# An xLSTM cell and a feed-forward block on one core: float64 weights narrowed another way, the causal mask added by TensorE, and a new order for the first group

## The chip, the cores and the metric

The kernel runs on one core of a Trainium2 chip. The core has a matrix engine (TensorE, PE in the profile; its weight loads are PEld), a vector engine (VectorE, DVE), an activation engine (ScalarE, ACT), GpSimd (POOL) and a queue processor (SyncE, SP) which here does nothing but issue DMA requests. The metric is the device time of one execution in microseconds.

## The reference

Two blocks follow each other. The first is a recurrent cell (mLSTM) over 4 batches, 8 heads, 768 time steps and a head width of 40; the second is a feed-forward block over the 3072 tokens that come out of it:

```python
for t in range(S):
    m_new = np.maximum(f_gate[:, :, t] + m, i_gate[:, :, t])
    f_stab = np.exp(f_gate[:, :, t] + m - m_new)
    i_stab = np.exp(i_gate[:, :, t] - m_new)
    C = f_stab * C + i_stab * np.einsum('bhd,bhe->bhde', vt, kt)
    n = f_stab * n + i_stab * kt
    y[:, :, t] = sigmoid(o_gate) * (C q) / np.maximum(np.abs(n q), 1.0)
h = x @ w_in                 # x: 3072 x 320, w_in: 320 x 2048
g = np.maximum(0.01 * h, h)
return g @ w_out             # w_out: 2048 x 320
```

All inputs are float32 but the two weights, which arrive as float64. No engine computes in 64 bits, so the kernel takes each float64 apart by its bits and makes a float32 of it ("narrowing").

## The kernel before, in words

The 768 time steps are cut into six chunks of 128. A *step* s is one chunk of one batch (s = 4 c + b), 24 in all. Inside a chunk the recurrence is written as matrix products: scores k q, weighted by exponentials of the gate sums under a causal mask, times v. The feed-forward block runs over *groups*: group g takes the four steps of chunk g (512 tokens). The work of group 0 (the feed-forward of chunk 0) is woven between the cells of chunk 1, that of group 1 between the cells of chunk 2, and so on.

A float64 quarter of w_in (320 x 512, 1.31 MB) is one unit to load and narrow, n = 0 to 3; a unit of w_out (256 x 320, 0.66 MB) is n = 4 to 11. `load_weights` issues a quarter of w_in as ten requests (five slots of two halves of the partitions; L230) and a unit of w_out as one (L235). `narrow_weights` (L248) is seven steps: ACT takes the absolute value of the top 16 bits (Abs, L260); DVE clamps it (L262), shifts the exponent (L264), puts the sign back (L266), masks the low 20 bits of the high word (L271), adds the scaled low word (L275) and multiplies with the exponent (L277).

Each engine runs its instructions in the order in which they are written (`tc.manual_schedule` for PE, DVE, ACT and POOL); SP's requests follow in about the same order. The start is written out by hand, as a string of short commands (ORDER, L1102). The commands that matter here:

- `ld s`: load k, q and v of a step; `lo s`: its output gate; `lw n`: a weight unit; `fd s`, `ll s i`: loads for the steps of later chunks (k, v and the gate rows spread over the partitions; q and o).
- `g c`, `ge c`, `ug c`: gate scans of a chunk on DVE, their exponentials on ACT, their transposes on PE.
- `ab s`: PE spreads the gate sums of steps s and s+1 over all partitions into four PSUM banks (`spread_first`); `abw s`: DVE adds the causal mask and writes the sum to SBUF (`spread_mask`, L471); `exp s`: 8 exponentials on ACT (L488), one for each head.
- `tr s i`, `tc s i`: transposes of k and q on PE and their copies out of PSUM; `sc`, `scm`: scores on PE, and their product with the exponentials on DVE (L600); `st`, `stc`: state on PE and its copy (L616); `vu`: v times gate on POOL.
- `val`, `den`, `gate`, `gp`: values on PE (L673), their denominators on DVE, the output gate on DVE (L685), the scaling on POOL (L702); `o`: the tanh of the output gate on ACT.
- `x s`, `xc s`: transposes of a step's result on PE (L876) and four copies on ACT (L889, L890), which make the x of the feed-forward block.
- `ff i`: the i-th of 32 units of group 0's feed-forward block. Units 0 to 15 are products with w_in (L907), each with two leaky relus on ACT (L915); units 0 to 3 use quarter 0 of w_in, 4 to 7 quarter 1, and so on; 0 and 1 need the x of steps 0 and 1, 2 and 3 that of steps 2 and 3. Units 16 to 31 are products with w_out (L942); 16 to 19 need weight units 4 and 5, and so on.
- `nw n`: the next step of narrowing unit n. `ps`: memsets of a state tile on POOL.

After the string (from L1151) a loop runs the other 30 ff units. Before unit i it issues PASSES[i] further narrowing steps, then, by the list `place`, the cells of chunk 1: `u_split` (k and q transposed, PE L564, copied by ACT L570), `split_qs` (scaled q, PE L550, ACT L552), `u_parts` (scores and states, PE L650 and L655, DVE L660 and L632), `u_plain` (values, PE L713). `ahead` prepares the next step: `prep_exp`, `prep_qs` (POOL L517), the loads, `state_next` (POOL L628), `prep_vu` (POOL L508) and `prep_mask` (POOL L480). From group 1 on another plan goes on, which is not touched.

PSUM has eight banks: four tagged `mm` (gate spreads, the products with w_in and w_out) and four tagged `c` (all else). A product whose bank is still being read waits, and with it all of PE's later work.

## Time and profile before

| | |
|---|---|
| median of 3 runs | 489.19 us (488.82 to 491.32) |
| span of the profiled execution | 489.4 us |
| PE busy | 476.1 us (97%) |
| DVE busy | 365.9 us (75%) |
| ACT busy | 197.4 us (40%) |
| POOL busy | 160.3 us (33%) |
| mean granted clock of PE | 0.982 |

The profiled execution is one of its own: its span is the time from its first to its last instruction. Busy time of PE includes the wait of a pipelined product for its place, so a busy PE is not at its peak. In the page's slices of the span the granted clock of PE (tenths of full speed, a 40th of the span each) stands beside the busy share of PE:

```profile
PE   7969998999999999999999999999999999999997
...
PEclk9867999999999999999999999999999999999999
```

A row of the table of stretches reads: start and end (us), the length, then for PE, PEld, DVE, ACT and POOL the busy time and the number of instructions, the granted clock, the busy share of the DMA engines, and GB/s. A row of the timeline: start, duration, engine, line, operation, output and inputs with their shapes, and the count.

### The profile page before, as it was taken

Reading aid. Unit: us, or ns where it says so; the run is one execution under the profiler, and the core shown is the slowest. Engines: PE = TensorE matmul, PEld = TensorE weight load, DVE = VectorE, ACT = ScalarE, POOL = GpSimd, SP = SyncE. Lnnn points to the kernel's source line nnn. Section 1 sums busy time; section 2 is a strip of 40 time slices with the busy share of each in tenths; the row PEclk is TensorE's granted clock in tenths of the full one; section 3 lists DMA queues with packets and bytes.
Section 4 is the critical chain, followed back from the end, with each engine's and each line's share of the span. In section 5 each row is a group of like instructions: output and inputs, shape, how many; then the busy total and the mean of one; then the engine's idle time right before and its main releaser. Section 6 shows DMA issues by size and latency. Waiting matters only on the chain.

```text
span 489.4 us, 12856 instructions
## 1 busy us (share of the span) xinstructions
PE 476.1 (97%) x5137; PEld 377.9 (77%) x5137; DVE 365.9 (75%) x595; ACT 197.4 (40%) x510; POOL 160.3 (33%) x207
## 2 busy tenths in 40 slices
PE   7969998999999999999999999999999999999997
PEld 6857887777745479975559995557998889988997
DVE  5796999799924999777898777679899968335611
ACT  4674885453642240324342141425024752156310
POOL 4234454070600725817280563644220002100020
PEclk9867999999999999999999999999999999999999
DMA  7777686898623566668787877755151030100001
GB/s 136 177 191 146 161 226 134 216 229 177 143 97 90 133 158 176 162 152 202 152 197 160 189 181 177 184 144 153 44 229 42 1 107 1 42 15 0 1 1 54
DMA packets 142699, 63.41 MB, mean 130 GB/s; under 512 B 110832, under 2 KB 130864, under 8 KB 142640
## 3 DMA queue, kind: packets, MB, share of 16 engines
q1 hardware_dynamic: 142256, 62.47, 52.7%
q8 instruction: 40, 0.66, 0.6%
q14 instruction: 19, 0.16, 0.1%
q10 hardware_dynamic: 384, 0.13, 0.1%
HBM read 51.68 MB, written 8.27 MB: 122 GB/s over the span
## 4 chain that ended last, share of the span: by engine, by line
PE 82%; SPq 8%; DVE 5%; issue 2%; DMA 2%; ACT 1%; ACTq 0%; DVEq 0%
PE po L983 32%; PE ph L907 24%; PE ph L833 8%; PE po L942 6%; PE pe L833 4%; PE pT L743 3%; PE sd L650 3%; SPq L230 3%; SPq L368 2%; SPq L377 1%; PE sd L655 1%; DVE w_in L275 1%; PE hN L713 1%; DMA raw<-in_moe_w_in_dram 1%; DVE late L266 1%
## 5 line engine op out<-in xcount | busy, mean ns | idle before, releaser
L907 PE MATMUL ph<-xT,w_in 64*128 64x512 f32 (+1 forms) x800 | 146.3, 516 | 0.2 <-ACT xT L889 0.2
L907 PEld LDWEIGHTS ph<-xT,w_in 64*128 64x128 f32 x800 | 77.8, 190 | 57.4 <-issue 50.8
L983 PE MATMUL po<-w_out,acts 128*128 128x160 f32 x640 | 91.0, 301 | 0.0
L983 PEld LDWEIGHTS po<-w_out,acts 128*128 128x128 f32 x640 | 87.5, 190 | 3.4 <-ACT w L488 1.5
L915 ACT ACTIVATE acts<-ph 128x512 f32<-128x512 f32 (+1 forms) x80 | 36.8, 508 | 83.6 <-PE ph L907 83.5
L488 ACT ACTIVATE w<-w,gT 128x64 f32<-128x64 f32 (+1 forms) x192 | 52.0, 349 | 29.0 <-POOL w L480 28.0
L628 POOL TENSOR_TENSOR S<-S,f 40x336 f32<-40x336 f32 x36 | 32.5, 902 | 93.3 <-PE pT L743 49.5
L983 PE MATMUL po<-raw,acts 128*128 128x160 f32 x320 | 45.1, 299 | 0.0
L983 PEld LDWEIGHTS po<-raw,acts 128*128 128x128 f32 x320 | 44.0, 190 | 0.0
L660 DVE TENSOR_TENSOR qn<-w,sd 64x512 f32<-64x512 f32 x40 | 27.4, 684 | 21.0 <-PE sd L655 14.0
L1016 POOL TENSOR_TENSOR y<-y,raw 128x160 f32<-128x160 f32 x10 | 5.5, 555 | 112.3 <-ACT y L1015 112.3
L942 PE MATMUL po<-w_out,acts 128*128 128x320 f32 x128 | 36.0, 436 | 0.0
L855 DVE SCALAR_TENSOR_TENSOR acts<-ph,acts 128x512 f32<-128x512 f32 x32 | 20.6, 684 | 20.7 <-ACT acts L853 20.7
L541 DVE TENSOR_TENSOR qn<-kqT,late 64x512 f32<-64x512 f32 x32 | 33.1, 1033 | 1.0
L480 POOL TENSOR_TENSOR w<-w,i 128x512 f32<-128x512 f32 x20 | 31.8, 1591 | 2.7 <-ACT acts L915 1.9
L942 PEld LDWEIGHTS po<-w_out,acts 128*128 128x128 f32 x128 | 23.8, 190 | 9.5 <-issue 0.3
L757 POOL TENSOR_TENSOR xb<-xb,den 128x320 f32<-128x320 f32 x16 | 11.6, 727 | 48.7 <-DVE xb L754 48.7
L853 ACT ACTIVATE acts<-pe 128x512 f32<-128x512 f32 x32 | 17.4, 594 | 19.2 <-PE pe L833 19.0
L761 DVE STREAM_TRANSPOSE x<-xb 128x512 f32<-128x512 f32 x16 | 17.8, 1114 | 7.7 <-POOL xb L757 7.7
L859 ACT ACTIVATE acts<-acts 128x512 f32<-128x512 f32 x32 | 19.7, 633 | 8.0 <-DVE acts L855 8.0
L983 PE MATMUL po<-raw 128*128 128x160 f32 x160 | 22.7, 300 | 0.0
L650 PEld LDWEIGHTS sd<-kqT 40*64 40x64 f32 x640 | 19.7, 135 | 3.7 <-issue 3.0
(166 smaller groups left out, 773.2 us busy)
## 6 DMA issues: line engine op xcount, KB each, us to landing
w<-a_dr SPq DMA_DIRECT2D x40, 128.0 KB, 3.7
rb<-in_k_dram SPq DMA_DIRECT2D x64, 80.0 KB, 3.1
rb<-in_q_dram SPq DMA_DIRECT2D x64, 80.0 KB, 2.7
rb<-in_o_gate_dram SPq DMA_DIRECT2D x64, 80.0 KB, 2.6
xT<-x_dr SPq DMA_DIRECT2D x32, 160.0 KB, 3.2
late<-a_dr SPq DMA_DIRECT2D x32, 128.0 KB, 3.4
x_dr<-x SPq DMA_DIRECT2D x16, 256.0 KB, 3.4
kn<-in_k_dram SPq DMA_DIRECT2D x24, 160.0 KB, 3.7
```

What stands on the lines that cost most here:

```text
L480: nc.gpsimd.tensor_tensor(w, w, cm2.unsqueeze(1).to_broadcast([P, H, SL]), op=ALU.add)
L488: yield nc.scalar.activation(w[:, h, :], w[:, h, :], AF.Exp, bias=gT[c][:, 0, bh : bh + 1], scale=1.0)
L541: nc.vector.tensor_tensor(mixed(s)[rows, 1 - r], d["kqT"][rows, 1].rearrange("p (h t) -> p h t", t=SL), d["ea"][rows], op=ALU.mult,)
L628: nc.gpsimd.tensor_tensor(new, old, g, op=ALU.mult)
L650: nc.tensor.matmul(bank[1 - u][toks, h, :], lhsT=kqT[rows, 0, ts(h, SL)], rhs=kqT[rows, 1, ts(h, SL)], start=True, stop=True,)
L660: nc.vector.tensor_tensor(mixed(s)[toks, u], w[toks], bank[1 - u][toks], op=ALU.mult)
L833: nc.tensor.matmul(ph[r][:], lhsT=parts["w", key][n][part, at : at + P], rhs=xs[key][part, slot, :], start=start and slot == 0, stop=stop ...
L855: nc.vector.scalar_tensor_tensor(fs[r], in0=ph[r][:], scalar=1.0 + EPS, in1=fs[r], op0=ALU.mult, op1=ALU.add,)
L907: nc.tensor.matmul(ph[r][:, cols], lhsT=w_row(r, slot, j), rhs=xT[DP * r : DP * (r + 1), slot, bs, :], start=(slot == 0), stop=(slot == KC ...
L915: nc.scalar.activation(acts[:, f, cols], ph[r][:, cols], AF.Prelu, alpha=0.01)
L942: nc.tensor.matmul(po[n][:], lhsT=acts[:, f, ts(n, P)], rhs=w_out[:, f, :], start=(f == 0), stop=(f == NF - 1),)
L983: nc.tensor.matmul(bank[:], lhsT=left[:, f, :], rhs=right[:, f, :], start=f == 0, stop=f == KH - 1)
```

## The change

Four things are changed together.

1. *Loads of w_in.* A quarter is requested in two pieces, one for each half of the partitions, all five slots at once. `lw n half` names the half; units of w_out stay whole.
2. *Causal mask.* `mask_first` (`mk s`) writes the mask into the four gate banks by a bf16 product with a bf16 identity, and the spreads of the gate sums are accumulated on top. `spread_mask` is gone. ACT's exponentials read the banks in PSUM themselves, two heads for each command (`exp s g`).
3. *Narrowing.* Six commands for each unit. `na`: Abs on ACT, clamp on POOL (flag 1) or DVE (0). `nr`: the exponent's shift, on ACT as a scaled identity (1) or on DVE (0). `ns`: the sign, on DVE. `ng`: the low word scaled and 2^20 added, as float32, on ACT (1) or POOL (0), so that its bits are an integer field. `nm`: the middle 16 bits times 8 are added to that field's lower half as an integer, on DVE. `nc`: exponent and sign are added to the upper half as 16-bit integers, on DVE. The three full-width passes L271, L275 and L277 are thus replaced by one pass on ACT or POOL and two on DVE. On ACT are nr 1, 4, 5, 7, 11 and ng 0, 4, 7 to 11; on POOL the clamps of na 1, 2, 7, 9, 11 and ng 1, 2, 3, 5, 6.
4. *Order.* All of group 0 is now in the string; the loop with `PASSES`, `place` and `ahead` is gone. Copies can be sent to ACT or DVE by a flag (`tc`, `stc`, `xc`): five of eight transpose copies are now on DVE, five of eight state copies on ACT. New commands name what `ahead` did: `us` (u_split), `qs`, `lz` (begin the exponentials), `ex s n` (n of them), `sn` (state_next), `tq` (split_qs), `up` (u_parts), `upl` (u_plain), `pm` (prep_mask), `kq`, `sq`, `pv`, `fi`, `ux` (x and its copies).

```diff
-    cmask = consts.tile([P, P], F32, name="cmask")
+    cmask = consts.tile([P, P], BF16, name="cmask")
...
+    ident_b = consts.tile([P, P], BF16, name="ident_b")
+    nc.vector.tensor_copy(ident_b[:], ident[:])
...
-            for slot in range(KC):
-                for r in range(2):
-                    nc.sync.dma_start(
-                        to[DP * r : DP * (r + 1), 2 * P * slot : 2 * P * (slot + 1)], src[r, :, slot, :],
-                    )
+            for r in range(2) if half is None else (half,):
+                nc.sync.dma_start(
+                    to[DP * r : DP * (r + 1), :].rearrange("p (k c) -> p k c", k=KC), src[r],
+                )
...
+    def narrow_abs(n, on):
+        w = narrow(n)
+        top, tops = w["t"].bitcast(BF16), w["tops"].bitcast(BF16)
         nc.scalar.activation(top, tops, AF.Abs)
+        eng = nc.gpsimd if on else nc.vector
+        eng.tensor_scalar(top, top, scalar1=2.0**-15, scalar2=122368.0, op0=ALU.max, op1=ALU.min)
+
+    def narrow_exp(n, on):
+        w = narrow(n)
+        w["sign"] = 0x8000 if on else 0xC000
+        if on:
+            nc.scalar.activation(w["t"], w["t"], AF.Identity, bias=exp_bias[:], scale=8.0)
+        else:
+            nc.vector.tensor_scalar(
+                w["t"], w["t"], scalar1=0x07FF, scalar2=3, op0=ALU.bitwise_and, op1=ALU.logical_shift_left,
+            )
+
+    def narrow_sign(n):
+        w = narrow(n)
         nc.vector.scalar_tensor_tensor(
-            t, in0=tops.bitcast(U16), scalar=0xC000, in1=t, op0=ALU.bitwise_and, op1=ALU.bitwise_or,
+            w["t"], in0=w["tops"], scalar=w["sign"], in1=w["t"], op0=ALU.bitwise_and, op1=ALU.bitwise_or,
         )
...
+    def narrow_low(n, on):
+        w = narrow(n)
+        if on:
+            nc.scalar.activation(w["dst"], w["lo"], AF.Identity, bias=low_bias[:], scale=2.0**-32)
+        else:
+            nc.gpsimd.tensor_scalar(w["dst"], w["lo"], scalar1=2.0**-32, scalar2=2.0**20, op0=ALU.mult, op1=ALU.add)
+
+    def narrow_mid(n):
+        w = narrow(n)
+        nc.vector.scalar_tensor_tensor(
+            w["dst"].bitcast(U32), in0=w["mid"], scalar=8.0, in1=w["down"], op0=ALU.mult, op1=ALU.add,
         )
...
+    def narrow_join(n):
+        w = narrow(n)
+        nc.vector.tensor_tensor(w["up"], w["up"], w["t"], op=ALU.add)
...
+    def mask_first(s2):
+
+        ab = st["ab", s2] = [psf.tile([P, 2, H // RG, P], F32, name=f"ab{r}", tag="mm") for r in range(RG)]
+        by = cmask[:].unsqueeze(1).to_broadcast([P, 2 * H // RG, P])
+        for r in range(RG):
+            nc.tensor.matmul(ab[r][:].rearrange("p n m t -> p (n m) t"), lhsT=ident_b[:], rhs=by, start=True, stop=False)
...
-                        rhs=a[rows, :], start=True, stop=True,
+                        rhs=a[rows, :], start=False, stop=n == 1 and m == H // RG - 1,
...
+    def exp_first(s, g):
...
+        for h in range(2 * g, 2 * g + 2):
+            bh = s * H + h
+            nc.scalar.activation(
+                w[:, h, :], ab[h % RG][:, n, h // RG, :], AF.Exp, bias=gT[0][:, 0, bh : bh + 1], scale=1.0,
             )
...
     ORDER = """
-ld 0; warm 12; ld 1; ld 2; lo 0; lo 1; lo 2; lw 0
-g 0; ld 3; lw 1; lw 2; lo 3; ge 0; ug 0; tr 0 0
...
+warm 12; ld 0 0; ld 0 1; ld 1 0; mk 0; lo 1; ld 1 1; ld 1 2; g 0; tiles; ld 0 2; tr 0 0; ge 0; ug 0
+vu 1; lo 0; ab 0; ld 2 0; tr 0 1; ld 2 1; tc 0 1 0; lw 0 0; lw 0 1; lw 1 0; tr 1 0; exp 0 0; ld 2 2
+exp 0 2; ld 3 0; tc 1 0 0; ld 3 1; exp 0 3; ld 3 2; exp 0 1; lw 1 1; tr 1 1; lw 2 0; vu 0; st 1
+tc 0 0 1; tc 1 1 0; exp 1 0; stc 1 1 1; stc 1 0 0; sc 0; scm 0 0; scm 0 1; lw 2 1; exp 1 2; st 0
+exp 1 1; stc 0 1 0; mk 2; exp 1 3; ab 2; exp 3 0; exp 2 0; o 0; g 1; ge 1; lo 3; sc 1; scm 1 0
+stc 0 0 0; scm 1 1; lo 2; val 0; tr 2 0; tr 2 1; den 0; val 1; exp 2 2; gate 0; tc 2 1 0; tc 2 0 0
+na 0 0; ps 1; den 1; ug 1; o 1; exp 3 1; gate 1; exp 2 1; sc 2; exp 2 3; ng 0 1; vu 2; scm 2 1; gp 0
+x 0; exp 3 2; xc 0 1; scm 2 0; st 2; stc 2 1 1; gp 1; x 1; tr 3 0; tc 3 0 1; tr 3 1; nr 0 0; stc 2 0 1
+na 1 1; val 2; tc 3 1 1; sc 3; ps 0; nm 0; ns 0; nc 0; exp 3 3; vu 3; xc 1 1; o 2; fd 4; ll 4 2
+ng 1 0; den 2; ff 0; st 3; scm 3 1; scm 3 0; stc 3 1 1; val 3; o 3; stc 3 0 1; nr 1 1; gate 2; gp 2
+x 2; xc 2 1; ff 1; ps 3; gate 3; den 3; gp 3; ng 2 0; x 3; nm 1; ns 1; xc 3 1; ll 4 1; fd 5; us 4
+qs 4; ps 2; pm 5; lw 3 0; ll 5 1; ff 2; lw 3 1; lw 4; fd 6; na 2 1; nc 1; nr 2 0; pm 4; lz 4; ll 6 0
+ff 3; ff 4; ns 2; vu 4; fd 7; ll 7 0; ex 4 3; ng 3 0; lw 5; lw 6; g 2; ex 4 3; ex 4 2; ff 5; ff 6
+sn 4 0; tq 4; up 4; qs 5; us 5; sn 5 0; ll 5 2; nm 2; ll 7 1; nc 2; na 3 0; nr 3 0; ll 6 1; ns 3; vu 5
...
+upl 7; ll 9 2; ll 9 1; ns 10; fd 11; ff 23; ff 24; nr 11 1; ff 25; lz 9; ns 11; nc 11; ff 26; pv 9
+nm 10; nc 10; ff 27; ff 28; kq 9; ll 11 1; ff 29; ux 5; ux 6; xb0; ll 11 0; ex 9 3; ex 9 3; ux 7
+ex 8 3; ex 8 3; vu 8; sq 11; fd 10; ex 8 2; ff 30; ff 31; sq 8; kq 8; ll 10 1; sq 10; ll 10 0; vu 9
+ex 9 2
 """
...
-        ffs = first_chunk()[2:]
-        fetch = {6: (3, 4), 17: (7,), 10: (5, 6)}
-        PASSES = (3, 2, 1, 0, 3, 5, 3, 1, 0, 1, 4, 2, 3, 4, 1, 2, 8, 4, 5, 4, 5, 4, 0, 7, 3, 5, 5, 1, 2, 8)
-        place = (1, 4, 7, 9, 11, 15, 15, 18, 23, 25, 27, 27, 28)
-        now = (None for n in range(2, QN + NF // 2) for _ in narrow_weights(n))
-        for i in range(len(ffs)):
-            run(now, PASSES[i])
...
+        first_chunk()
```

More of the change, by code (lines that the diff above doesn't have):

```diff
@@ L212, in load_weights @@
         to = dst
-        if wide:
+        if wide and half == 1:
+            to = raws[n][0]
+        elif wide:
             if n < 2:
@@ new lines, in narrow @@
+    def narrow(n):
+        if n not in words:
+            raw, dst = raws[n]
+            pair = raw.bitcast(U32).rearrange("p (c two) -> p c two", two=2)
+            four = raw.bitcast(U16).rearrange("p (c four) -> p c four", four=4)
+            words[n] = dict(
+                lo=pair[:, :, 0], mid=four[:, :, 2], tops=four[:, :, 3], t=halves(n, dst.shape[1]).bitcast(U16), dst=dst,
+                down=dst.bitcast(U16).rearrange("p (c two) -> p c two", two=2)[:, :, 0],
+                up=dst.bitcast(U16).rearrange("p (c two) -> p c two", two=2)[:, :, 1],
+            )
+        return words[n]
```

198 lines of the change are left out of this document (56 added, 142 removed).

## The prediction

> **What bounds the kernel now.** I read the stretches first (time, busy time of PE, PEld, DVE, ACT and POOL, granted clock, DMA share, GB/s), because group 0 is all that the change touches.
>
> ```profile
> 6.10:20.90 14.80, 12.37 (x184) 10.73 (x184) 11.36 (x35) 10.00 (x30) 2.81 (x9) 1.00 0.90 182
> 20.90:33.50 12.60, 12.04 (x90) 10.31 (x89) 10.04 (x19) 9.12 (x25) 5.75 (x11) 0.66 0.76 181
> ...
> 37.40:47.10 9.70, 9.70 (x67) 7.43 (x64) 5.82 (x10) 3.19 (x9) 3.29 (x8) 0.77 0.73 142
> 47.10:91.00 43.90, 42.39 (x815) 37.19 (x816) 40.90 (x53) 32.74 (x85) 20.73 (x18) 1.00 0.78 188
> 91.00:135.20 44.20, 43.65 (x382) 31.44 (x378) 40.73 (x62) 20.43 (x53) 18.10 (x18) 1.00 0.82 179
> 135.20:489.00 353.80, 350.99 (x3570) 276.04 (x3570) 250.30 (x399) 117.55 (x306) 105.14 (x128) 1.00 0.44 112
> ```
>
> From 135.2 us (group 1) to the end PE never rests: there is nothing to win there. From 47.1 to 135.2 PE is idle for 2.1 us. The loss lies before 47.1: PE idles and runs at clock 0.5 to 0.77, and only two of 32 ff units are done. The chain of waits names the cause in order of time:
>
> ```profile
> 20.04 0.59 SPq L230
> ...
> 21.94 2.57 SPq L368
> 24.55 2.51 DMA acts<-in_moe_w_in_dram
> 27.12 0.41 DVE late L264
> 27.55 0.98 DVE late L266
> ```
>
> SP's queue issues w_in in requests of 0.6 us, ten to a quarter, and DVE narrows what landed. The waits before 47.1 show where PE stands: on the x copies of ACT, ahead of the first ff unit (it starts at 37.45 by the timeline).
>
> ```profile
> PE dC L608 <- ACT xT L890: 3.3, 1, 3.3
> ...
> ACT late L260 <- DMA raw<-in_moe_w_in_dram: 2.0, 1, 2.0
> ```
>
> How much is there at most: PE's own work until 135.2 is 36.0 (L942) + 16 half units at 2.25 (four in 4.50 in the chain) = 36.0 + cells of chunk 0, about 25 at full clock (transposes 4.8, gate spreads 2.3, scores 4.6, values 7.9, xt 2.8, rest 2.6) + cells of chunk 1, 4 x 4.4 + 0.7 = 18.3: together 115.4. From PE's first data at 6.1 that is 121.5, against 135.2. So 13.7 us are the ceiling.
>
> **The change part by part.**
>
> *w_in in two requests.* 32 of 40 issues of 0.6 us fall away: 19 us of SP's queue, 13 of them before 37.4 (ending quarter 2). Now w_in 0 follows 10 small loads instead of 12. The bytes stay. In 26 to 36 us the engines moved 201 to 217 GB/s at a share of 0.70 to 0.80, so there is room when requests are ready. With 1.31 MB a quarter at 180 to 280 GB/s: w_in 0 lands at 18 to 20 (about 24.5 now), w_in 1 at 26 to 31 (33.5 now), w_in 2 at 31 to 37. I take 19, 29 and 34: DMA then no longer stands before ACT's second Abs.
>
> *Mask by PE.* DVE loses 16 additions, 5.6 us (L471). PE gains 2 x 4 bf16 products of 512 columns. No such product is in the trace. An f32 product here is two instructions, each 281 ns for 320 columns (L942, 16 in 4.50 in the chain); a bf16 one as long as one of those, scaled to 512 columns, is 450 ns, the upper end, and half of it the lower: 0.9 to 1.8 us per call, 0.9 taken at full clock. mk 0 lies in the wait for data; mk 2 lies before ab 2, which now cannot start until the last exponential of step 1 has freed the banks: ACT ends it near 14.7, ab 2 near 16.3 (14.4 now). So PE's cells run 1 to 2 us later than now until val 1. The exponentials read PSUM: 0.306 us each stays (bounds 0.25, by the slope between L915 at 256 and L570 at 512 columns, and 0.35).
>
> *Narrowing.* Undisturbed rows of w_in:
>
> ```profile
> 26.16 0.49 DVE L262 TENSOR_SCALAR late<-late 128x1280 bf16<-128x1280 bf16 x1
> ...
> 27.08 0.44 DVE L264 TENSOR_SCALAR late<-late 128x1280 uint16<-128x1280 uint16 x1
> ...
> 31.47 1.49 DVE L275 SCALAR_TENSOR_TENSOR w_in<-acts,w_in 128x1280 f32<-128x1280 uint32 x1
> ...
> 38.89 1.49 DVE L266 SCALAR_TENSOR_TENSOR late<-acts,late 128x1280 uint16<-128x1280 uint16 x1
> ...
> 45.13 0.80 DVE L271 TENSOR_SCALAR w_in<-acts 128x1280 uint32<-128x1280 uint32 x1
> ```
>
> With L277 (1.49) that is 6.2 us; w_out, half as wide, 3.6. Four and eight of them: 53.5. After, DVE keeps three two-input passes (ns, nm, nc; 1.49 and 0.82 as L266, since all walk a tensor in steps): 4 x 4.5 + 8 x 2.5 = 37.6, and 5.3 of clamps and shifts left to it: 42.9. DVE's balance: -10.6 (narrowing), -5.6 (mask), +3.2 (five transpose copies at 0.64, as L600), -1.7 (five state copies to ACT) = -14.7 us of 116 in group 0. ACT's: nr 1.4 + 4 x 0.8, ng 1.4 + 6 x 0.8 (L260's 1.37 and 0.80; a 32-bit stepped input could cost twice that), state copies +2, transposes -2.6: about +10 on 80. POOL: ng and na, five of 1280 columns and five of 640. Its one-input copy of 64x320 takes 0.47 beside nothing (a pair in 0.94) and one of 64x64 0.26: 0.82 ns a column, so 1.3 us for 1280; its two-input row, 0.73 for 320, gives 2.9. I take 1.6, between, nearer the one-input row: 12 us on 55 in group 0, and POOL's waits for PE and DVE are the cover.
>
> *The order, first stage.* ACT is what now sets ff 0. From ab 0's end near 9.0 (as now plus 0.1 for mk 0): 32 exponentials 9.8, three transpose copies 1.6, three state copies 1.2, two tanh 0.9, ge 1 1.1, two Abs 2.7, ng 0 1.4, two x copies 3.4 = 22.1, plus 2 us in which it waits for ab 2: 33.1. DVE's list up to nc 0 (copies 4.2, mixes 3.8, gates of chunk 1 2.7, denominators and gates 2.3, w_in 0 5.4) is 18.4 us from 6.8, and ends near 32 with the late inputs of its mixes. PE's work up to there is 22 us at full clock from 7, but at the half clock of 20.9 to 33.5 it would end at 35. I take 34.2 for ff 0, with bounds 32 and 36.5: -3.2 us. Between ff 0 and us 4 the same work follows in the same order (ff, st 3, val 3, ff, x 2, x 3): 9.65 as now. Had PE the full clock there, 2.3 less (ff 0 takes 4.61 at half, 2.25 at full clock).
>
> *Second stage.* PE's waits from 47.1 on are these:
>
> ```profile
> PE hN L713 <- DVE S L632: 1.0, 1, 1.0
> PE tg L342 <- DVE hn L724: 0.4, 1, 0.4
> PE hN L713 <- DVE qn L660: 0.3, 1, 0.3
> ...
> ```
>
> All of DVE's are narrowing standing before a step's state add. With 10 us less on DVE and chunk 1's loads issued earlier I take half back, -1.0 (bounds -1.9 and +1.5: ACT's narrowing passes stand before relus, of which PE can hold only two pairs of banks). SP: the loads of chunk 1 are no longer behind w_in 3. At the seam to group 1 the x copies of steps 5 to 7 and 6 exponentials, 6.9 us of ACT, lie beside ux 5 to 7, ff 30 and ff 31, 5.7 us of PE: up to 1 us, inside those bounds.
>
> Sum: 489.4 - 3.2 - 1.0 = 485.2 for the profiled execution, whose span stands 0.2 above the median of the runs: **485.0**.
>
> **A rule against it.** POOL and DVE stretch each other in this trace:
>
> ```profile
> 48.96 1.97 POOL L517 TENSOR_TENSOR y<-rb,gT 128x320 f32<-128x320 f32 x1
> ...
> 99.92 0.72 POOL L517 TENSOR_TENSOR y<-rb,gT 128x320 f32<-128x320 f32 x1
> ```
>
> ```profile
> 33.00 1.49 DVE L277 SCALAR_TENSOR_TENSOR w_in<-w_in,late 128x1280 f32<-128x1280 f32 x1
> ...
> 47.91 2.44 DVE L277 SCALAR_TENSOR_TENSOR w_in<-w_in,late 128x1280 f32<-128x1280 f32 x1
> ```
>
> The two lines of each pair are the same instruction with the other engine at rest and at work (POOL's L480 and L517 run from 47.7 to 50.9). The Trainium skill, "SBUF — State Buffer", section "Who interferes with whom", says that a DVE instruction with two SBUF inputs and a GpSimd one that reads SBUF exclude each other for a whole instruction. The trace agrees (1.97 against 0.72). By it the three passes that stay on DVE would each block POOL's new ones; the price by rows is in the slower rival.
>
> **The rivals.**
> 1. *PE stays dense and at full clock* (faster still). For it: PE waits for DMA, DVE and ACT in turn now, and the first two are relieved. Against: the clock fell at 20.9 although PE was 84% busy before, with small products that remain. ff 0 at 32 (-5.4), ff 0 at full speed (-2.3), second stage -1.9: 479.6. The Trainium skill, "TensorE: Matmul & The Clock Gate", Part 1, has the clock halved after an idle window and restored after about 3.4 us of sustained work; the trace agrees for the return (ff 0 began at 37.45, the clock was full again near 41).
> 2. *The transfers were hidden anyway* (no change). ACT's chain of 22 us and PE's half-clock cells set ff 0 whatever lands when; ab 2 two us later and w_in 1's Abs ahead of the second x copy eat the gain. ff 0 at 36.5, the second stage +0.5: 488.8. For it: PE had only 0.56 us of rest in 20.9 to 33.5. Against: ACT waited 2.0 us for w_in 1 itself, and 1.4 before w_in 0's Abs.
> 3. *POOL becomes the wait* (slower). Between 32 and 60 us POOL gets five passes of 1280 columns beside 12.3 us of old work (x scalings, memsets, masks, vu, states), and gp 2, gp 3 and the masks of chunk 1, for which PE waits before x 2, x 3 and the parts, queue behind ng 1 to ng 3. At 1.6 us it has 8 us to spare; at 3.1 each the 28 us are full, and from there each 0.1 costs 0.5. If blocking stretches the 1.6 by the 2.7 times of L517, to 4.3, that is 6 us, plus 2 for the state updates of DVE behind it, less the gain of 3.2: 494. Against: POOL's own rest in 47.1 to 91.0 is 23 us.
>
> **How the numbers follow.** Forecast 0.47 (its own range 482.5 to 486.7), rival 1 0.17, rival 2 0.18, rival 3 0.18. Half a per cent is 2.4 us, about what a measurement here can tell. Faster: rival 1 and nearly all of the forecast, 0.62; within: 0.20; slower: 0.18. The range leaves out half of rival 1's lower side and most of rival 3: 480.3 to 491.0.
>
> **What would show it.** Right: the first ff unit starts at 34 +- 1.5; SP's queue has 8 w_in requests and the second Abs no longer waits for DMA; group 1's first ff begins near 131; DVE busy 14 us less until then, ACT 10 more, POOL 12 more. Wrong: POOL's passes above 3 us with PE waiting on x scalings, or relus late on ACT so that PE stands between 50 and 100 us; and on the other side a clock of 1.00 from 20 to 45.

## The result, and the profile after

The changed kernel takes 511.78 us (median of 4 runs, 510.04 to 512.77) against 490.25 (488.82 to 491.4) for the kernel before on the same chip: a ratio of 1.043, 95% interval [1.040, 1.047]. It is slower by 21.5 us; 485.0 was predicted, and 491.0 was the upper end of the range. The profiled execution spans 511.0 us (489.4 before).

The stretches of the changed kernel, with the columns as before (length, busy time of PE, PEld, DVE, ACT, POOL, granted clock, DMA share, GB/s), the first four cut like those of before:

```profile
6.10:20.90 14.80, 13.08 (x172) 10.11 (x170) 6.87 (x18) 7.86 (x29) 2.45 (x7) 0.88 1.32 172
20.90:33.50 12.60, 7.14 (x74) 6.32 (x74) 10.78 (x20) 7.01 (x17) 5.80 (x6) 0.75 1.05 172
37.40:47.10 9.70, 9.70 (x77) 8.55 (x77) 2.53 (x6) 5.18 (x15) 8.70 (x9) 0.64 0.83 123
47.10:91.00 43.90, 38.50 (x660) 32.28 (x659) 31.20 (x37) 29.72 (x70) 28.49 (x25) 0.92 0.82 174
...
156.80:510.60 353.80, 350.98 (x3570) 276.02 (x3570) 250.73 (x400) 119.84 (x315) 105.30 (x128) 1.00 0.46 113
```

The last row has the length and PE's 3570 products of the last row of before, to the hundredth: group 1 begins at 156.8 instead of 135.2, and those 21.6 us are the whole loss. It splits at the first transposes of step 4, which start the second stage: 51.2 us here, 47.1 before. So the first stage loses 4.1 us and the second 17.5. One row for the second stage of each kernel, the changed one and then the one before:

```profile
51.20:156.80 105.60, 93.93 (x1195) 74.07 (x1194) 70.54 (x96) 58.34 (x137) 51.82 (x46) 0.94 0.66 147
```

```profile
47.10:135.20 88.10, 86.04 (x1195) 68.63 (x1194) 81.62 (x115) 53.16 (x137) 38.84 (x36) 1.00 0.80 184
```

The same 1195 products. PE idles 11.7 us (2.1 before), and its busy time is 7.9 us longer, at a mean clock of 0.94: 9.6 us more rest came with 7.9 us more busy time, of which the clock accounts for some 6 (an estimate: 0.06 of 105.6 us). The DMA engines moved no more bytes for it (105.6 us at 147 GB/s against 88.1 at 184), and DVE, relieved as intended, is busy 11 us less: it waits.

PE's waits in the changed kernel (total, times, longest):

```profile
PE xt L914 <- POOL x L740: 6.2, 3, 5.1
PE sd L693 <- POOL vu L547: 3.3, 2, 2.4
PE ph L945 <- ACT acts L953: 2.4, 1, 2.4
PE tk L603 <- ACT qn L591: 1.8, 2, 1.7
PE tk L603 <- DMA rb<-in_q_dram: 1.6, 1, 1.6
```

POOL comes first; before, PE's waits named it only for constants that it sets up at the start (`ident` and `i`, 1.5 and 1.4 us). Its timeline shows why, in two places:

```profile
27.96 0.72 POOL L537 TENSOR_TENSOR vu<-S,gT 128x320 f32<-128x320 f32 x1 [2.88 <-DMA S<-in_v_dram]
...
29.07 3.93 POOL L740 TENSOR_TENSOR x<-x,den 128x320 f32<-128x320 f32 x2
...
57.74 1.27 POOL L519 TENSOR_TENSOR w<-w,i 128x512 f32<-128x512 f32 x1 [1.38 <-DMA w<-a_dr]
59.09 4.51 POOL L275 TENSOR_SCALAR late<-late 128x1280 bf16<-128x1280 bf16 x1
63.58 1.27 POOL L519 TENSOR_TENSOR w<-w,i 128x512 f32<-128x512 f32 x1
```

In the first stage the scaling of step 0's result (L740, `gp 0`) stands behind step 2's `vu` (L537), which waits for step 2's v; that load is now asked for behind one and a half quarters of w_in and arrives at 28. PE's 5.1 us before x 0 are this. In the second stage step 4's mask (the second L519) stands behind step 5's and behind a clamp of a weight unit of 4.51 us. Its exponentials, in the timeline of ACT, have waited 4.97 us, and a relu of four instructions waits behind them:

```profile
64.89 2.02 ACT L527 ACTIVATE w<-w,gT 128x64 f32<-128x64 f32 x8 [4.97 <-POOL w L519]
66.81 1.17 ACT L953 ACTIVATE acts<-ph 128x256 f32<-128x256 f32 x4
```

Theory from here: four engines and SP each run their list in order, and the new list puts commands that wait for a load or for a slow pass ahead of commands that PE needs. Rivals: the new passes themselves are too dear; the larger requests; the mask; PE's own new sequence.

### The profile page after: what moved, and what is told of

It is laid out like the page before. It is cut to its first block, busy times and chain, and to the rows that moved or that the text cites. A ratio compares the mean times of both kernels' runs of the same rounds, so it can differ in the third digit from the quotient of the medians.

```text
span 511.0 us, 12782 instructions
## 1 busy us (share of the span) xinstructions
PE 486.7 (95%) x5145; PEld 385.7 (75%) x5145; DVE 349.2 (68%) x558; ACT 205.4 (40%) x522; POOL 181.8 (36%) x219
## 3 DMA queue, kind: packets, MB, share of 16 engines
q1 hardware_dynamic: 141744, 62.47, 54.7%
## 4 chain that ended last, share of the span: by engine, by line
PE 75%; POOL 6%; DMA 5%; SPq 4%; DVE 4%; ACT 3%; issue 3%; ACTq 0%; POOLq 0%; DVEq 0%
PE po L1021 30%; PE ph L945 23%; PE ph L871 7%; PE pe L871 4%; PE pT L781 3%; PE sd L688 3%; DMA S<-in_v_dram 3%; POOL late L275 2%; POOL w L519 2%; DMA w<-a_dr 1%; POOL x L740 1%; SPq L398 1%; PE pa L711 1%; DVE w_out L308 1%; PE sd L693 1%
## 5 line engine op out<-in xcount | busy, mean ns | idle before, releaser
L945 PE MATMUL ph<-xT,w_in 64*128 64x512 f32 (+1 forms) x800 | 149.8, 525 | 3.3 <-ACT acts L953 2.4
L945 PEld LDWEIGHTS ph<-xT,w_in 64*128 64x128 f32 x800 | 81.5, 196 | 60.7 <-issue 50.9
L527 ACT ACTIVATE w<-w,gT 128x64 f32<-128x64 f32 x160 | 41.7, 340 | 36.1 <-POOL w L519 36.0
L698 DVE TENSOR_TENSOR qn<-w,sd 64x512 f32<-64x512 f32 x40 | 27.4, 684 | 36.4 <-PE sd L693 15.1
L980 PE MATMUL po<-w_out,acts 128*128 128x320 f32 x128 | 38.2, 452 | 1.7 <-DVE w_out L308 1.3
L519 POOL TENSOR_TENSOR w<-w,i 128x512 f32<-128x512 f32 x20 | 32.8, 1638 | 7.0 <-DMA w<-a_dr 6.9
L795 POOL TENSOR_TENSOR xb<-xb,den 128x320 f32<-128x320 f32 x16 | 11.7, 729 | 48.6 <-DVE xb L792 48.6
L275 POOL TENSOR_SCALAR late<-late 128x640 bf16<-128x640 bf16 (+1 forms) x5 | 16.1, 3210 | 20.9 <-ACT late L273 20.8
L693 PE MATMUL sd<-S,vu 64*40 64x42 f32 x576 | 19.7, 215 | 3.3 <-POOL vu L547 3.3
```

What stands on the lines that cost most here:

```text
L275: eng.tensor_scalar(top, top, scalar1=2.0**-15, scalar2=122368.0, op0=ALU.max, op1=ALU.min)
L519: nc.gpsimd.tensor_tensor(w, w, cm2.unsqueeze(1).to_broadcast([P, H, SL]), op=ALU.add)
L527: yield nc.scalar.activation(w[:, h, :], w[:, h, :], AF.Exp, bias=gT[c][:, 0, bh : bh + 1], scale=1.0)
L693: nc.tensor.matmul(dC[u][:, h].rearrange("p k d -> p (k d)"), lhsT=d["ku"][toks, h], rhs=S_v[s % NL][toks, u, h, :, :V1], start=True, stop ...
L698: nc.vector.tensor_tensor(mixed(s)[toks, u], w[toks], bank[1 - u][toks], op=ALU.mult)
L945: nc.tensor.matmul(ph[r][:, cols], lhsT=w_row(r, slot, j), rhs=xT[DP * r : DP * (r + 1), slot, bs, :], start=(slot == 0), stop=(slot == KC ...
```

## The experiments

Two times tell where a run stands: when step 4 begins its transposes, and when group 1 begins (profiled execution, us). "Stage 2" is the difference. They are of one execution, whose own time lies up to 2 us beside the kernel's median (in a_fix_q, further down, 3.2 us above it), so that small differences between stages say little; the ratio is of all executions.

| kernel | step 4 | group 1 | stage 2 | ratio to before [95%] |
|---|---|---|---|---|
| before | 47.1 | 135.2 | 88.1 | 1 |
| changed | 51.2 | 156.8 | 105.6 | 1.0432 [1.0398, 1.0466] |
| a_clamp | 52.0 | 152.4 | 100.4 | 1.0378 [1.0326, 1.0429] |
| a_ten | 49.7 | 151.9 | 102.2 | 1.0393 [1.0345, 1.0441] |
| a_oldnarrow | 51.8 | 151.1 | 99.3 | 1.0337 [1.0283, 1.0390] |
| b_two | 46.1 | 134.1 | 88.0 | 0.9984 [0.9968, 0.9999] |
| b_narrow | 50.6 | 138.2 | 87.6 | 1.0082 [1.0055, 1.0109] |
| b_twomask | 46.3 | 134.4 | 88.1 | 1.0025 [1.0002, 1.0049] |
| b_all | 50.6 | 138.2 | 87.6 | 1.0094 [1.0067, 1.0121] |
| h_loop | 49.5 | 138.6 | 89.1 | 1.0085 [1.0063, 1.0108] |

### One part alone, or one part undone

**Clamps back on DVE** (a_clamp). In the changed kernel's list:

```diff
-na 1 1; ... na 2 1; ... na 7 1; ... na 9 1; ... na 11 1
+na 1 0; ... na 2 0; ... na 7 0; ... na 9 0; ... na 11 0
```

> The changed kernel with all twelve clamps on DVE (none on POOL). Theory P (POOL is the wait: its five clamps of 4.51 and 2.34 us hold back masks, vu and state updates): the chain of waits of the changed kernel has 11.5 us of clamps, so 500 to 503 us. Theory L (the order of the loads: v of step 2 lands 13.3 us after its issue because w_in 0 and half of w_in 1 are ahead of it): 508 to 511, the first ff unit still starts at 40.9.

Measured: 508.66 us, inside the range of theory L; the ratio falls by 0.54 of a per cent, 2.6 us, with intervals that still overlap. In the profiled execution the second stage gains 5.2 us and the first loses 0.8 (why, further down). The clamp takes 4.51 us for 1280 columns on POOL and 2.34 for 640, on DVE 0.49 and 0.33 where nothing disturbs it (up to 1.05 and 0.84 elsewhere).

**Ten requests again** (a_ten), in `load_weights` of the changed kernel, at the same places of the list:

```diff
-            for r in range(2) if half is None else (half,):
-                nc.sync.dma_start(... all five slots ...)
+            for slot in range(KC):
+                for r in range(2) if half is None else (half,):
+                    nc.sync.dma_start(... one slot ...)
```

> The changed kernel with w_in in ten requests of 128 KB a quarter, at the same places of the order. Theory S (large requests as such hold back the small ones): v of step 2 lands 4 us or more earlier and the time falls to 506 or less. Theory L (their place in the order and the bandwidth): the same 512, v of step 2 again lands near 28.

Measured: 509.85; 1.0393 and the changed kernel's 1.0432 have intervals that overlap. Step 2's v arrives at 27.4 instead of 28.0 and PE's wait for `gp 0` is 4.5 us instead of 5.1: the size of the requests is not the main cause. The same part in the kernel before, alone (b_two):

> The kernel before with w_in in two requests a quarter and nothing else. Theory S: slower, 493 or more. Theory L (SP's issues were not the limit, the engines' bandwidth was): 488.5 to 491. The prediction's view (SP's queue was the limit): 487 to 488.5, w_in 1 landing 2 us or more earlier than 33.5.

Measured: 490.04, ratio 0.998, some 0.8 us gained. The Abs of w_in 1 begins at 33.4 (33.55 before), not 2 us sooner, as it would had SP's queue been the limit. It is the only kernel here that is faster than the one before, and the interval ends at 0.9999.

**The new arithmetic alone** (b_narrow): the kernel before with the new passes in the old places, clamps and shifts on DVE, the low word with the Abs on ACT (units 0, 4, 7 to 11) or POOL (1, 2, 3, 5, 6).

```diff
-        nc.vector.tensor_scalar(d, hi, scalar1=0x000FFFFF, scalar2=0x00100000, ...)
-        nc.vector.scalar_tensor_tensor(dst, in0=lo, scalar=2.0**-32, in1=d, ...)
-        nc.vector.scalar_tensor_tensor(dst, in0=dst, scalar=2.0**-20, in1=top, ...)
+        (scalar.activation or gpsimd.tensor_scalar)(dst, lo, ... 2.0**-32, 2.0**20)
+        nc.vector.scalar_tensor_tensor(dst.bitcast(U32), in0=mid, scalar=8.0, in1=down, ...)
+        nc.vector.tensor_tensor(up, up, t, op=ALU.add)
```

> The kernel before with the new arithmetic of narrowing in the old places: the low word on ACT (units 0, 4, 7 to 11) or POOL (1, 2, 3, 5, 6) together with Abs, clamps and shifts all on DVE. If the arithmetic is a gain as predicted (DVE less by 8 us undisturbed), 486.5 to 489; if its passes are stretched by POOL's reads, 491 or more.

Measured: 495.02, 0.8% slower where a gain had been predicted, and all of it ahead of step 4 (50.6 against 47.1; the second stage is 0.5 us shorter than before). Part of this is not arithmetic; the section on the hardware says what it is.

**Requests and mask** (b_twomask), and **everything but the order** (b_all: the same and the new arithmetic, in the old list and loop). `0..3` stands for four commands:

```diff
-ab 0; abw 0; ... exp 0; ... abw 1; ... exp 1; ... ab 2; ... abw 3; ... abw 2; ... exp 2; ... exp 3
+mk 0; ab 0; exp 0 0..3; ... exp 1 0..3; ... mk 2; ab 2; ... exp 3 0..3; ... exp 2 0..3
```

> The kernel before with two requests per quarter of w_in and with the mask summed in PSUM; the old arithmetic and the old order. VectorE loses 8 mask passes of the first steps, and ScalarE reads the exponentials' input from PSUM. Theory: these two are small gains, 487 to 490.5. Rival: the two banks that are held until the exponentials of both steps are done delay the products behind them: 491 to 494.

> The kernel before with three parts of the change and without the fourth: w_in in two requests per quarter, the new arithmetic (clamps and shifts on VectorE), the mask summed in PSUM by bf16 products and the exponentials read from there; all in the old order and the old loop. Theory: the order carries the loss: 490 to 496 (495.0 for the arithmetic alone, 0.7 less for the requests, up to 2 less for the mask). Rival: the parts together stall TensorE whatever the order: 503 or more.

Measured: 491.75 and 494.74. Relieving DVE of the mask gains nothing (1.0025 against 0.998 for the requests alone; the theory of a small gain fell). Three parts of the change together cost 0.94%; the fourth, the order, takes that to 4.3%. The order, with the engines that it names for the passes, carries some 17 us.

**The order, with the old passes** (a_oldnarrow): the changed kernel's list, in which `na`, `nr`, `ng`, `nm`, `nc` issue the old instructions on DVE.

> The changed kernel, its order of commands untouched, with the old arithmetic in it: each of the six commands of a unit issues the old pass on VectorE (only the absolute value stays on ScalarE), so no pass is on GpSimd and no other on ScalarE. Theory: the list's order itself is what is slow, and spreading the passes over three engines gave back little: 506 to 514, since VectorE gains some 14 us of work and has some 90 us idle before group 1. Rival: passes on GpSimd and ScalarE, in line with the cells' work there, stall TensorE: 493 to 500.

Measured: 506.06. With no pass on POOL, and on ACT only the Abs, the list is still 3.4% slower; its second stage takes 99.3 us, 11.2 more than before. So most of the second stage's loss needs none of the new passes.

**The new first stage, the old second** (h_loop): the string up to the first transposes of step 4, then the old loop (`PASSES`, `place`, `ahead`) with the passes of b_narrow, so with the clamps and shifts of units 2 to 11 on DVE.

```diff
-ng 2 0; x 3; nm 1; ns 1; xc 3 1; ll 4 1; fd 5; us 4
-qs 4; ps 2; pm 5; lw 3 0; ... (the rest of the string)
+x 3; nm 1; ns 1; xc 3 1; ll 4 1; fd 5; nc 1
+ps 2; ll 5 1; lw 3; lw 4; lw 5; lw 6; fd 6; fd 7; ll 5 2
```

> The changed kernel's list up to the first transposes of step 4 (the whole first stage, with its narrowing of w_in 0 and 1), and behind it the old loop of the kernel before, which places the cells of steps 4 to 7, the loads and the passes of units 2 to 11 by its own tables; the passes there are the new ones, clamps and shifts on VectorE as in the run of the new arithmetic alone (495.0). Theory: the second half of the new list carries most of the loss (from step 4's transposes to group 1 it took 105.5 us in the changed kernel against 88.1 before, and 17.4 of the 21.6 us lie there): 495 to 500, with the 4 us of the first stage left and group 1 beginning near 141. Rival: the second stage is slow because of what the first hands over (late w_in, transfers piled up), whatever list follows: 505 to 512.

Measured: 494.66. Taking back the second part of the list returns 17.1 of 21.5 us. Its second stage, to be held beside the two rows above:

```profile
49.50:138.60 89.10, 86.19 (x1196) 68.50 (x1195) 80.59 (x107) 57.45 (x144) 47.69 (x40) 1.00 0.84 182
```

The same work, behind the same list for the first stage, with the new arithmetic, takes 1.0 us longer than before and not 17.5. So the loss of the second stage comes neither from the arithmetic in itself nor from what the first stage hands over, but from how the new list arranges it; a part of that is where it puts the passes (6.3 us less in a_oldnarrow, 5.2 in a_clamp, each in one execution).

### Which commands of the list

**Five commands moved** (a_fix, on a_clamp). The profile of a_clamp gives the chains. POOL, then ACT, at PE's longest wait:

```profile
87.10 0.72 POOL L556 TENSOR_TENSOR y<-rb,gT 128x320 f32<-128x320 f32 x1 [6.39 <-DMA rb<-in_q_dram]
...
88.75 1.73 POOL L519 TENSOR_TENSOR w<-w,i 128x512 f32<-128x512 f32 x1
90.56 1.21 POOL L298 TENSOR_SCALAR w_out<-w_out 128x640 f32<-128x640 uint32 x1
91.85 1.75 POOL L519 TENSOR_TENSOR w<-w,i 128x512 f32<-128x512 f32 x1
```

```profile
93.64 0.82 ACT L527 ACTIVATE w<-w,gT 128x64 f32<-128x64 f32 x3 [5.57 <-POOL w L519]
94.49 1.21 ACT L953 ACTIVATE acts<-ph 128x256 f32<-128x256 f32 x4
```

Step 7's scaled q (`qs 7`, L556) is listed early and waits 6.4 us for its load. Behind it stand step 7's mask, a weight pass and step 6's mask (the last L519); step 6's exponentials wait for that, two relus for them, and PE (idle 4.83 us until 94.92) for the relus' banks. A load that nothing needs yet stops three engines.

```diff
-ps 2; pm 5; lw 3 0; ... na 2 0; nc 1; nr 2 0; pm 4; lz 4; ... ns 2; vu 4; fd 7
+ps 2; pm 4; vu 4; lw 3 0; ... nc 1; na 2 0; nr 2 0; lz 4; ... ns 2; pm 5; fd 7
-tq 5; qs 7; nr 4 1; ... pm 7; ng 5 0; nm 5; pm 6; lz 6; ... qs 6; upl 5
+tq 5; nr 4 1; ... pm 6; ng 5 0; nm 5; pm 7; lz 6; ... qs 6; qs 7; upl 5
```

> The changed kernel with its clamps on VectorE (508.7 by itself), and five commands of the second stage moved that stand at the head of an in-order queue and wait: the join of unit 1 ahead of the clamp of unit 2 (whose absolute value waits for a load), step 4's mask and vu ahead of step 5's mask on GpSimd, step 6's mask ahead of step 7's, and step 7's scaled q, which there waited 6.4 us for its load on GpSimd, behind step 6's. TensorE's list is left as it is. Theory: what is slow in the new list are these heads, through GpSimd to the exponentials on ScalarE and the Prelus behind them (4.8 us of TensorE's idle time at 90 to 95 us, 4.8 at 58 to 63, and a lower clock behind each): 496 to 502. Rival: TensorE's own sequence of cells and feed-forward units is too tight for the latencies of the cells, and other waits take the place of these: 505 to 510.

Measured: 503.43, 1.0262 [1.0234, 1.0291], a little above the forecast (496 to 502). Step 4 at 53.4, group 1 at 147.4: the second stage falls from 100.4 to 94.0, the first becomes 1.4 us longer.

**And step 6's q earlier** (a_fix_q): `ll 6 1` moved from behind step 7's loads to ahead of `fd 6`.

> The run with five moved commands (503.4) with one more: the load of step 6's q is asked for before step 6's k and v instead of behind them and behind step 7's; SP stood 10 us on those, and TensorE waited 3.6 us for this q at 82 us, with the clock at 0.77 of full speed over 75 to 90 us. Theory: what is left of the second stage's loss (94.0 us from step 4's transposes to group 1 against 88.1 before) is this one load: 497 to 500, and the second stage 88 to 90 us long. Rival: the next wait takes its place: 502 to 505.

Measured: 499.06, 1.0162 [1.0134, 1.0191], as forecast. But the profiled execution, at 502.30 us the slowest of the four (from 497.23), has its second stage at 94.9 us (51.5 to 146.4), not 88 to 90: the wait for this q is gone from the rows and one of 2.8 us for the narrowing of w_out is there instead. So the theory's number held and its reason is not shown; how long the second stage took in the faster executions no profile shows.

**The first stage's commands** (a_loads, on the changed kernel):

```diff
-ld 2 1; tc 0 1 0; lw 0 0; ... exp 0 0; ld 2 2
+ld 2 1; ld 2 2; tc 0 1 0; lw 0 0; ... exp 0 0
-vu 2; scm 2 1; gp 0
+gp 0; vu 2; scm 2 1
```

> The changed kernel with three commands of the first stage moved: v of step 2 is asked for ahead of w_in's first quarter instead of behind one and a half quarters, and on GpSimd the gate's scaling of steps 0 stands ahead of step 2's v. Theory: the first stage's loss (first transposes of step 4 at 51.2 against 47.1 us) hangs on the chain v of step 2, its scaling, the gate's scaling of step 0, x 0; TensorE's 5.1 us there go, and the rest of the stage follows by some 2 to 4 us: 507 to 510. Rival: w_in 0 then lands later by the v that goes first and the narrowing sets ff 0 instead: 511 to 513, no gain.

Measured: 509.84, 1.0395 [1.0365, 1.0425]: inside the forecast, but the interval overlaps that of the changed kernel. PE's wait before x 0 is gone; step 4 begins at 50.6, only 0.6 us sooner: w_in's two Abs now begin at 24.8 and 36.3 (24.0 and 36.2), and step 2's tanh still waits 3.6 us for its output gate on ACT. So the chain that I had named was not, by itself, what bound the stage. In the hybrid, with unit 1's clamp on DVE as well (h_v2), and with the old arithmetic (h_old):

> The changed first stage with the old loop behind it (494.7), with the same three commands moved and unit 1's clamp on VectorE instead of GpSimd (4.5 us there, with step 3's v behind it). Theory: the first stage is a chain of in-order waits on GpSimd; without them step 4's transposes begin 2 to 4 us sooner than 49.5 and all behind them as well: 490.5 to 492.5. Rival: the arrival of w_in and its narrowing bound the stage: 494 to 495.5.

> The same as the run before it, with the old arithmetic in all units (all passes but the absolute value on VectorE). The new arithmetic alone cost 0.8% in the old order, all of it ahead of step 4. Theory: that cost comes from the passes that ScalarE and GpSimd take over there, so the old arithmetic gives 1 to 4 us less than the run before it: 487 to 490.5, perhaps the fastest of all. Rival: VectorE then has more to do ahead of ff 0 and it is no faster: 491 to 494.

Measured: 498.42 and 496.71 (1.0160 and 1.0124), 3.8 and 2.1 us slower than h_loop. Both forecasts fell. DVE's timeline of h_v2:

```profile
37.71 0.49 DVE L275 TENSOR_SCALAR late<-late 128x1280 bf16<-128x1280 bf16 x1 [7.74 <-ACT late L273]
38.12 1.49 DVE L302 SCALAR_TENSOR_TENSOR w_in<-acts,w_in 128x1280 uint32<-128x1280 uint16 x1
...
41.04 1.62 DVE L308 TENSOR_TENSOR w_in<-w_in,late 128x1280 uint16<-128x1280 uint16 x1
```

The cheap clamp (0.49 us) of unit 1 waits 7.7 us for its Abs, so for w_in's second quarter, and unit 0's last three passes, which could have run, stand behind it. On POOL unit 1's clamp was dear, but no pass of unit 0 stood behind it on DVE. The same wait stands in a_clamp (7.1 us) and a_fix (7.9). Moving this clamp behind unit 0's last pass, in the hybrid (h_v3) and in the repaired list (a_fix2):

```diff
-na 1 0; val 2; ... nm 0; ns 0; nc 0; ... ng 1 0; den 2; ff 0
+val 2; ... nm 0; ns 0; nc 0; ... ng 1 0; den 2; na 1 0; ff 0
```

> The changed first stage with the old loop, commands moved as in the run that gave 498.4, and unit 1's clamp moved behind unit 0's last pass on VectorE. Theory: that clamp was what made that run 3.8 us slower than the one with the clamp on GpSimd (494.7): 489 to 492.5, step 4's transposes at 46.5 to 49 us. Rival: asking for step 2's v first is what cost it: 496 to 499.

> The run before it, with the three commands of the first stage moved (step 2's v ahead of w_in, gate's scaling of step 0 ahead of step 2's v on GpSimd) and unit 1's clamp on VectorE moved behind unit 0's last pass: in the runs with the clamps on VectorE it stood there 7.7 us for unit 1's absolute value, so for the load of w_in's second quarter, with unit 0's last three passes behind it. Theory: with these heads gone the first stage too is as before, step 4's transposes at 47 to 49.5 us: 490 to 494 in all, the whole loss back with the new arithmetic and TensorE's new list unchanged. Rival: the arrival of w_in bounds the first stage: 496 to 499.

Measured: 500.07 and 501.83 (1.0196 and 1.0230), not faster than h_v2 and slower than a_fix_q. Yet ff 0 began at 36.0 in h_v3, earlier than in the kernel before (37.45). What followed, on ACT:

```profile
35.16 0.37 ACT L962 COPY xT<-xt 64x256 f32<-64x256 f32 x1
43.22 0.47 ACT L595 ACTIVATE acts<-acts 128x320 f32<-128x320 f32 x1 [7.69 <-DMA acts<-in_o_gate_dram]
43.59 1.32 ACT L273 ACTIVATE late<-acts 128x1280 bf16<-128x1280 bf16 x1
```

Step 2's tanh (`o 2`) waits for an output gate that the new list asks for behind w_in, with the Abs of w_in 1 behind it. Asked for earlier (h_v4 and a_fix3):

```diff
-ld 2 2; tc 0 1 0; lw 0 0; ... lw 1 1; ... ge 1; lo 3; sc 1; ... scm 1 1; lo 2; val 0
+ld 2 2; lo 2; tc 0 1 0; lw 0 0; ... lo 3; lw 1 1; ... ge 1; sc 1; ... scm 1 1; val 0
```

> The run before in the hybrid (500.1; there feed-forward unit 0 began at 36.0 us, ahead of the 37.5 of the kernel before, and step 4's transposes at 55.9) with the loads of the output gate for steps 2 and 3 asked for ahead of w_in's first and second quarter; there they stood behind one and a half quarters more, and step 2's landed at 43.2 us, when ScalarE had stood 7.7 us on its tanh, with the absolute value of w_in's second quarter, the Preluse of unit 0 and step 3's tanh behind it. Theory: ScalarE's queue head was what was left of the first stage's loss: step 4's transposes at 47 to 49.5 us, 488.5 to 493. Rival: the order in which w_in and the rest land only moves the wait: 496 or more.

> The changed kernel's whole list with all moves of commands so far and these two loads. Theory: as for the hybrid, and with the second stage repaired (89 to 95 us in the two runs with the q moved): 490 to 496, so nearly the whole loss of 21 us back without a change in TensorE's list or in the new arithmetic. Rival: 498 or more.

Measured: h_v4 494.48 (1.0082 [1.0060, 1.0103]), 5.6 less than h_v3, so this head is shown; but with step 4 at 49.4 it is no better than h_loop and some 4 us above the kernel before, short of the forecast. a_fix3 502.88 (1.0248 [1.0226, 1.0270]): step 4 at 48.9, 7.7 sooner than in a_fix2, and no gain in all, against the theory. The four repaired lists, from step 4 to group 1: 53.4 to 147.4, 51.5 to 146.4, 56.6 to 145.8, 48.9 to 146.3. The second stages of the last two:

```profile
56.60:145.80 89.20, 86.42 (x1195) 68.34 (x1194) 70.79 (x99) 58.15 (x138) 44.64 (x41) 1.00 0.74 164
```

```profile
48.90:146.30 97.40, 89.65 (x1196) 70.30 (x1195) 70.18 (x101) 58.30 (x138) 44.22 (x42) 0.96 0.78 163
```

Beginning late, PE's new sequence runs as dense as the old loop (2.8 us of rest in 89.2), so the sequence is not too tight in itself. Beginning 7.7 us sooner it loses those us again: 5.0 us more rest and 3.2 us more busy time, at a mean clock of 0.96. By the first product with w_out the two are level (102.7 in a_fix2, 103.1 in a_fix3), so the loss lies ahead of it. In a_fix3 PE waits there for step 4's q (2.1 us), w_in 2's last pass (1.0) and 2.8 us, until 85.96, for which the profile names nothing. Something other than PE's start seems to hold group 1 near 146 in these; it is no fixed limit, since a_fix_q, whose median is 3.2 us below its profiled execution, would by that begin it near 143 (an estimate). Which of the list's loads or passes it is, is not settled.

**The kernel before, with step 3's output gate earlier** (b_lo, on b_two):

```diff
-g 0; ld 3; lw 1; lw 2; lo 3
+g 0; ld 3; lo 3; lw 1; lw 2
```

> The kernel before with two requests per quarter of w_in (490.0, a ratio of 0.998) and with one command moved: the output gate of step 3 is asked for behind step 3's k, q and v, ahead of w_in's second and third quarter; in the kernel before ScalarE stood 3.9 us on it at 40.5. Theory: the same queue head binds the kernel before a little: 487.5 to 489.5, faster than both. Rival: ScalarE's 3.9 us are covered by TensorE's work on unit 0, and the load ahead of w_in's second quarter takes 0.9 us from it: 490 to 491.

Measured: 491.24, 1.0011 [0.9998, 1.0025]: no gain, against the theory; ff 0 at 39.3 and step 4 at 48.3. Its clock was 0.50 from 21 to 42 us, where b_two had 0.72 in 20.9 to 33.5 (below).

## Why the prediction was wrong

The step that failed is the second stage: forecast at -1.0 us, it took +17.5. The first stage went wrong too, with +4.1 where -3.2 was forecast. The terms in turn:

**"There is room when requests are ready": w_in 0 at 19, w_in 1 at 29.** Measured: the Abs of w_in 0 began at 24.0 and that of w_in 1 at 36.2, both after a wait for DMA (24.75 and 33.55 before). I read the share of 0.70 to 0.80 as room. In b_two, the same requests alone, the share went from 0.90 to 1.08 in 6.1 to 20.9 us and the rate from 182 to 198 GB/s; from 27 to 36 us a share of 1.04 to 1.06 moved 208 to 212 GB/s, no more than the 201 to 217 in which I had seen room. The issue time was no limit that mattered: rival 2, "the transfers were hidden anyway", was right on this part, which is worth 0.8 us.

**ff 0 at 34.2.** Measured 40.9 (37.45 before). The sum added up ACT's work and let each queue run as soon as its engine was free. It had no term for a queue that waits at its head. `gp 0` behind `vu 2` behind a load was in the list, to be read there; so was `o 2` behind `lo 2` (ACT waited 3.2 us on it in the changed kernel, and 7.7 in h_v3, where the first was mended).

**"Between ff 0 and us 4 9.65 as now."** 10.3 measured; in h_v3, where the output gate was late, 19.8. It is no constant.

**Second stage, -1.0 (bounds -1.9 and +1.5).** Measured +17.5. It took the new list to be as good as the old loop and counted the relief of DVE. DVE was relieved by more than I said (98.5 us busy until group 1 instead of 115.6, so -17.1 against -14.7), and it bought nothing: before, PE rested 2.1 us in this stage, so 2 us was all there was to gain and everything to lose. h_loop shows that the list is the cause, and a_fix that some 6 us of it are heads of queues (100.4 to 94.0); a_oldnarrow, without the new passes, still has 11.2 of the 17.5. What the rest is (94.0 to 97.4 us in three of the four mended lists, 89.2 in the one that began late) stays open, and so do the 4 us that h_loop and h_v4 lack: the shift of the tiles told below and the half clock (0.50 from 30 to 40 us in h_v4) are in them, in shares that no run parts.

**POOL's passes at 1.6 us (bounds 1.3 and 2.9).** Mis-sized where it hurt: the low word took 1.36 to 2.49, but the clamp 4.51, beyond the bound. (The 2.49 stood beside two DVE passes that took 2.03 and 2.69 instead of some 1.5 and 1.6, so the engines do stretch each other, by 1.8 times there and not 2.7.) POOL's balance was +21.3 us, not +12; ACT's +5.8, not +10. a_clamp measures the price of the clamps: 2.6 us in all, 5.2 in the second stage of the profiled execution. So rival 3 named the place, and its worst price (4.3 a pass) was reached, but by the operation itself: it is 4.51 at 37.6, when DVE is at rest for most of the stretch, and at 59.1, when DVE does nothing from 54.7 to 63.6. The sign of being wrong that the prediction named, passes above 3 us with PE waiting on x scalings, came true in both halves, though PE's longest such wait (5.1 us) hung on step 2's v and not on these passes.

**The mask.** `mk` took 1.0 and 1.7 us (0.9 taken, 1.8 the bound); b_twomask gained nothing by the passes that DVE was spared.

**Small readings.** PE does rest behind 135.2, for 2.8 of 353.8 us by the row shown. Its work until there adds up to 115.3, not 115.4. The clock, read as full again near 41, was at 0.50 until 41 and 0.55 from 41 to 42, so it returned near 41.9, 4.4 us after ff 0 began. None of these enters the forecast's sum.

## What to carry to other kernels

Where engines run hand-written lists in order, cost a new order by its queue heads: for each command that waits for a load or another engine, name what is listed behind it on that engine and who needs that, before adding up busy times. Do not relieve an engine for which PE waits only 2 us in a stage of 88; a change there has little to win and much to lose: here 9.6 us more rest of PE came with 7.9 us more busy time. And before adding a constant, look at where it pushes the tiles that DMA writes.

## What the runs showed of the hardware

**Two small constants slowed the loads.** The new arithmetic needs `low_bias` (and `exp_bias`): 4 bytes a partition, which take 32 and shift every tile behind them. In the compiled programs k's tile starts at byte 136288 of a partition before and in b_twomask, 136320 in b_narrow, 136352 in the changed kernel and all made from it; that is 96, 128 and 160 beyond a multiple of 256. Each head's row of k, q or v is 160 bytes at a pitch of 256. The stretch from 6 to 15 us and the median time of k's loads (last column, us) for before, b_twomask, b_narrow and a_oldnarrow:

```profile
6.00:15.00 9.00, 7.29 (x140) 6.19 (x142) 5.76 (x18) 7.05 (x22) 2.81 (x9) 1.00 1.06 181
...
kn<-in_k_dram SPq DMA_DIRECT2D x3, 160.0 KB, 3.3
```

```profile
6.00:15.00 9.00, 6.87 (x75) 5.26 (x74) 0.93 (x3) 5.71 (x20) 2.81 (x9) 0.95 1.09 189
...
kn<-in_k_dram SPq DMA_DIRECT2D x4, 160.0 KB, 3.4
```

```profile
6.00:15.00 9.00, 6.86 (x103) 5.69 (x102) 4.25 (x11) 6.39 (x19) 2.65 (x9) 0.96 1.53 139
...
kn<-in_k_dram SPq DMA_DIRECT2D x3, 160.0 KB, 5.2
```

```profile
6.00:15.00 9.00, 6.84 (x87) 5.58 (x88) 2.53 (x5) 4.76 (x18) 2.45 (x7) 0.88 1.50 148
...
kn<-in_k_dram SPq DMA_DIRECT2D x4, 160.0 KB, 4.8
```

In this stretch the kernels without the constants (before, b_two, b_lo, b_twomask) have a share of 1.05 to 1.09 and 181 to 191 GB/s; all those with them (b_narrow, b_all, the changed kernel and the thirteen made from it) 1.40 to 1.53 and 139 to 151. b_narrow has the old order of loads, a_oldnarrow the old arithmetic: only the constants, and the shift that they bring, are common. At 96 a row of 160 bytes ends at a multiple of 256; at 128 and 160 it crosses one. The Trainium skill, "DMA: Bandwidth & Descriptors", section "How a descriptor splits into AXI transactions", says, of reads, that a descriptor is cut at multiples of 256 bytes. If that holds for these writes too, a row would be one transaction before and two after, which fits the rows. That the boundary is the reason is argued, not shown: no kernel with the constants in another place was tried. What it cost: in b_narrow the request for step 3's k came 2.2 us later (22.84 against 20.68) and the first Abs 1.9 us later, before any new pass had run, of the 3.5 us that its step 4 was late.

**The clock can stay at half through 15 us of busy rows.** In b_lo, three of five such rows in sequence:

```profile
21.00:24.00 3.00, 3.00 (x17) 2.92 (x17) 0.49 (x2) 3.00 (x11) 0.68 (x2) 0.50 0.87 130
...
27.00:30.00 3.00, 3.00 (x26) 2.60 (x27) 2.90 (x8) 1.31 (x4) 0.95 (x2) 0.50 1.06 232
...
33.00:36.00 3.00, 3.00 (x22) 2.70 (x22) 2.94 (x3) 1.48 (x1) 0.00 (x0) 0.50 1.06 218
```

PE counts as busy for all 15 us, rests for most of 36 to 39, and the clock returns only in its first feed-forward unit, which began at 39.3: it is 0.50 until 42, 0.80 in 42 to 43 and 1.00 behind. The prediction cited the Trainium skill, "TensorE: Matmul & The Clock Gate", Part 1, for a return after some 3.4 us of sustained work; the feed-forward unit fits that, the small products of the cells do not, if a busy row is taken for sustained work. Busy time includes waits of pipelined products, and what the clock needs was not tested.

**max and min on GpSimd are slow.** 4.51 us for 1280 bf16 columns (3.5 ns a column) and 2.34 for 640, while multiply and add with a change of type took 1.36 for 1280 (1.06 ns) undisturbed. The same clamp on DVE takes 0.49 undisturbed.
